# Mamba-2 scan and mixture of experts on one core: GpSimd waits for VectorE's turn on the shared port, first loads reordered and held back, sums of logarithms made in the opening

## The chip, the cores and the metric

The kernel runs on one core of a Trainium2 chip. The core has five engines with instruction queues of their own: TensorE (PE, matrix products from SBUF into PSUM; its weight loads are shown as PEld), VectorE (DVE), ScalarE (ACT), GpSimd (POOL) and SyncE (SP, which here issues nearly all DMAs). Engines wait for each other by semaphores; each works through its queue in order, so that one waiting instruction holds everything behind it. The metric is the device time of one execution in microseconds. Three executions of the kernel before gave 621.44, 622.16 and 623.01 us; the median is 622.16.

## The reference

Two blocks follow each other. The first is a state-space scan over 4 sequences and 8 heads, 768 positions each, head dimension 32, state dimension 16, in chunks (the kernel uses chunks of 128 positions, the result is the same):

```python
log_a = np.log(np.clip(a, 1e-06, 1.0))
cum = np.cumsum(la, axis=-1)                       # within a chunk
L = np.exp(cum[:, :, :, None] - cum[:, :, None, :]) * causal
M = np.einsum('bhin,bhjn->bhij', Cc, Bc) * L
y_intra = np.einsum('bhij,bhjd->bhid', M, xc)
y_inter = np.einsum('bhin,bhnd->bhid', Cc, state) * np.exp(cum)[:, :, :, None]
y[:, :, sl] = y_intra + y_inter
Bx = np.einsum('bhjn,bhjd->bhjnd', Bc, xc) * np.exp(cum[:, :, -1:] - cum)[:, :, :, None, None]
state = decay_full[:, :, None, None] * state + np.sum(Bx, axis=2)
```

The second is a mixture of four experts over the 3072 tokens of 256 values that the first makes, with hidden size 1024 and probabilities `p` normalised over the experts:

```python
for e in range(E):
    h = np.maximum(x @ w1[e], 0.0)
    out += p[:, e:e + 1] * (h @ w2[e])
```

All is float32.

## The kernel before

**Tiles.** The 24 chunks of 128 tokens are numbered so that four neighbours belong to the four sequences. A chunk's data come in `xb` (x, B and the transposes of B and C). The decay matrix of a chunk is made in one of two ways. For chunks 0 to 5 (`SCANNED`) DVE makes it by a running product of the decays (`scan`, L513 and L515), for chunks 0 to 2 from decays that PE has spread over the partitions, for 3 to 5 from a tile `ab` that a DMA spreads from the DRAM copy `acut_d` of the clipped decays (L457 to L460). For chunks 6 to 23 ACT makes it as an exponential (L522) of `ab`, spread from `cum_d`, the DRAM copy of the running sums of logarithms, minus the transposed sums `neg`; GpSimd then sets the upper triangle to zero (`causal`, L527). From chunk 4 on the state carried in is scaled by `dec` (L829: the exponential of `ah`, loaded from `cum_d` at L465) into `cts` (GpSimd, L831). PE multiplies C by B (`score`, L498), DVE multiplies the result by the decay matrix (L847), PE makes the outputs (L542 and, for the carried state, L870), ACT copies them out (L885 and L552), DVE transposes and carries the state (L901 and L903). `fade` (L536, GpSimd) scales B.

**The experts** are worked through in products of 128x256 blocks by a scheme with fewer products than the plain one. It needs sums of weight blocks (`w`, L1015, by GpSimd or DVE), sums of token blocks (`Y`, L1034, DVE), and sums of products (DVE: L951, L1062, L1251 and L1424). The first four chunk pairs' worth of work is done with smaller schemes: four plain products (`plain_first`), whose outputs go to the `own_` house, then two pairs of feature blocks (`twos`), then units of four feature blocks (`fours`) over blocks of six chunks. All products are issued at L924, each as a pair of matrix multiplications. ACT copies intermediate results out of PSUM (L933, L1204 and L1208) and back into it (L938); DVE applies the rectifier and the gate (L959). Sums of weights that later blocks need again are stored (`w_d`, L1020) and loaded again (L1004).

**What sets the order.** Up to L727 the order is the program's own: the opening. It loads the first tiles, clips the decays, makes chunks 0 and 1 and the gates; ACT copies the transposed gates at L643, and at L671 the scores that GpSimd multiplies; DVE multiplies the other scores at L677. From there on every piece of work is an entry (`Work`) with the engines that may do it, a duration in the planner's own cost table, and what it reads and writes. PE's entries stand in an order written out by hand (`line`). `Plan.run` then goes through time, and gives each free engine the ready entry with the earliest due time (`latest`), counted back from PE's order; it also chooses the tile. It knows DVE's and GpSimd's shared port: entries of DVE with `two` (both inputs in SBUF) and of GpSimd with `port` do not overlap in the plan (`self.port`). The instructions are issued in the order of planned starts (L1506 to L1509). On the chip only true dependencies make an engine wait, so that the plan's times do not hold anything back there.

**SP's queue.** SP issues the loads and stores in the planned order. Eight semaphores serve them in turn, so a DMA is not issued before the one eight places earlier has landed. The first part is the program's own: `xb` of chunks 0 and 1, two tiles of `w1` (L473), `xb` of chunk 2, the store of `acut_d` (L626), `xb` of chunk 3, `ab` of chunk 3, two more tiles of `w1`, four of `w2` (L479). From `p_d` (L727), the DRAM copy of the gates, on it is the plan's order.

**The sums of logarithms.** After the sixth entry of `line` (`MARK`) ACT takes the logarithm of the decays in place (L1378), DVE makes the running sums in two scans (L1380), SP stores them to `cum_d`. `bias()` transposes them by PE into `neg`; it stands after the fifth of the `twos` products (L1413 to L1415).

Of the kernel before, what the change touches and what calls it, by code (L numbers as in the profile page):

```python
# [36 lines left out]
SCORED, OWN, LEAD, LEFT, MARK = 5, 3, 5, 3, 5  # L37
FILLED = 3
ORDERS = (0, 1, 2, 3), (3, 1, 2, 0), (0, 1, 2, 3), (3, 1, 2, 0)
# [29 lines left out]
class Plan:  # L69
# [109 lines left out]
    def run(self, line, at, begin):  # L179
# [19 lines left out]
        while todo:  # L199
# [4 lines left out]
            for w in waiting[e]:  # L204
                if w.start is not None or e == "PE" and w.place != head:
                    continue
# [149 lines left out]
def kernel(  # L356
# [100 lines left out]
    def load_decays(c, ab):  # L457
        src = acut_d if c < SCANNED else cum_d
        nc.sync.dma_start(
            out=ab, in_=src[real(c)].rearrange("h s -> (h s)").partition_broadcast(P))  # L460
# [16 lines left out]
    def load_w2(fb, w):  # L477
        e, f = divmod(fb, EPB)
        nc.sync.dma_start(  # L479
            out=w.rearrange("p (j m) -> p j m", j=JJ),  # L480
            in_=w2[e, f * FB:f * FB + FB].rearrange("(j p) m -> p j m", p=P))
# [149 lines left out]
    load_decays(3, homes["ab"][0])  # L631
    for fb in range(2, 4):
        load_w1(fb, homes["W"][fb])
    for fb in range(4):
        load_w2(fb, homes["W"][4 + fb])

# [66 lines left out]
    turn_gates(BANK[7])  # L703
    next_ = [BANK[4], BANK[0], BANK[1], BANK[6]]
# [11 lines left out]
    for r in (3, 1, 2):  # L716
        masked(1, r, MT[1], LT[1], next_[r], 0)
    ys = []
# [52 lines left out]
    la = plan.taken("cum", 0, now)  # L771
    cum, neg, cd = value("cum"), value("neg"), value("dram")
    cd.dram = True
# [598 lines left out]
    for seq, _ in plain[:2]:  # L1372
        line.extend(seq)
    scores([2, 3])
    for seq, _ in plain[2:]:
        line.extend(seq)
    mark = line[MARK]
    act(.42, lambda e: nc.scalar.activation(out=la.t, in_=la.t, func=AF.Ln), part=[la], after=mark)  # L1378
    for r in range(2):
        dve(.6, lambda e, r=r: nc.vector.tensor_tensor_scan(  # L1380
            out=cum.t[:, r], data0=la.t[:, r], data1=zeros[:NCH * NH // 2], initial=0.0,
            op0=ALU.add, op1=ALU.add), two=True, reads=[la], part=[cum], after=mark)
    dma(lambda e: store_decays(nc.sync, cum_d, cum.t), kb=96, reads=[cum], part=[cd])
# [29 lines left out]
    line.extend(rest[:5])  # L1413
    bias()
    line.extend(rest[5:])  # L1415
# [86 lines left out]
    for i, w in enumerate(leave_last(len(blocks) - 1, O, LAST)):  # L1502
# [3 lines left out]
    done = plan.run(line, now, {"PE": now, "DVE": now - .6, "ACT": now + 1.0, "POOL": now - 2.0,  # L1506
                                "SP": now + 1.0})
    for w in done:
        w.fn(w.by)  # L1509

# [44 lines left out]
```

## Time and profile before

| | us |
|---|---|
| median of three executions (621.44 to 623.01) | 622.16 |
| the profiled execution's own time | 624.35 |
| its span, first to last instruction | 622.6 |
| PE busy in the span | 606.6 |
| DVE busy | 498.7 |
| ACT busy | 291.7 |
| GpSimd busy | 180.9 |
| DVE busy in the window 13 to 150 (137 us) | 121.3 |
| GpSimd busy in the window 13 to 150 | 91.3 |

In the lines of the profile, `L924 PE MATMUL bank<-v,w ... x8` is an operation of PE that was written in line 924, reads tiles `v` and `w` and writes `bank`, eight times. In a timeline the first number is the start, the second the length of the group; in brackets stands how long the engine was idle before it and what ended that. A list of waits gives the time in total, the number of times and the longest. PE's matrix multiplications are pipelined: one of 128x256 in float32 lasts 381 ns, and the next starts 216 ns after it; each product at L924 makes four. PEclk is the granted clock of PE in tenths, in 40 slices of the span of 15.6 us each.

### The profile page before, as it was taken

What the parts mean: (1) busy time and instruction counts of PE and PEld (TensorE: products, weight loads), DVE (VectorE), ACT (ScalarE), POOL (GpSimd) and SP (SyncE); (2) the same over time, 40 slices, a digit from 0 to 9 for tenths busy, and PEclk for the clock granted to TensorE, in tenths of its full rate; (3) what the DMA queues carried; (4) which work ended last, traced back from release to release, by engine and by line L of the source; (5) the groups of instructions that cost most, each with busy time, mean ns of one, the idle gap of its engine ahead of it and who ended that gap; (6) DMA issues with size and microseconds to landing.
All of it is one profiled execution on the core that took longest, in us unless ns stands there. A gap on an engine that the chain in (4) does not pass through costs nothing.

```text
span 622.6 us, 10073 instructions
## 1 busy us (share of the span) xinstructions
PE 606.6 (97%) x3365; PEld 515.1 (83%) x3365; DVE 498.7 (80%) x852; ACT 291.7 (47%) x681; POOL 180.9 (29%) x240
## 2 busy tenths in 40 slices
PE   9979989989999999999999999999999999999997
PEld 5757868868888888888888888888888888888885
DVE  6879897998879987497877989487695988576675
ACT  4247627357662325867534332855435142444441
POOL 6586962973262110696700110110000000000000
PEclk9999989999999999999999999999999999999999
DMA  6968538636772526976352332974233232974001
GB/s 185 322 211 269 176 110 274 218 125 220 271 249 68 163 35 183 326 263 239 102 159 78 106 103 50 298 247 141 82 93 94 83 103 34 307 232 130 1 0 52
DMA packets 89060, 99.65 MB, mean 160 GB/s; under 512 B 27428, under 2 KB 58928, under 8 KB 89008
## 3 DMA queue, kind: packets, MB, share of 16 engines
q1 hardware_dynamic: 88852, 98.95, 50.7%
q8 instruction: 27, 0.44, 0.3%
q14 instruction: 25, 0.20, 0.1%
q10 hardware_dynamic: 156, 0.06, 0.0%
HBM read 78.80 MB, written 20.17 MB: 159 GB/s over the span
## 4 chain that ended last, share of the span: by engine, by line
PE 82%; DVE 8%; DMA 5%; issue 2%; POOL 1%; ACT 1%; SPq 0%; DVEq 0%; POOLq 0%; ACTq 0%
PE bank L924 79%; DVE v L951 2%; DVE v L959 1%; DMA ah<-cum_d 1%; DMA ab<-acut_d 1%; POOL w L1015 1%; DMA w<-in_w_dram 1%; PE bank L498 1%; PE bank L542 1%; DVE Y L1034 1%; DMA acut_d<-v 1%; DVE w L1015 1%; DVE MT L847 1%; DMA ab<-cum_d 1%; PE bank L870 0%
## 5 line engine op out<-in xcount | busy, mean ns | idle before, releaser
L924 PE MATMUL bank<-v,w 128*128 128x256 f32 x1672 | 394.7, 381 | 5.2 <-DVE v L959 2.5
L924 PEld LDWEIGHTS bank<-v,w 128*128 128x128 f32 x1672 | 317.3, 191 | 53.0 <-issue 4.8
L924 PE MATMUL bank<-Y,w 128*128 128x256 f32 x692 | 177.7, 381 | 4.2 <-DVE bank L1062 1.8
L924 PEld LDWEIGHTS bank<-Y,w 128*128 128x128 f32 x692 | 130.0, 190 | 26.1 <-DVE bank L1062 2.4
L1204 ACT COPY v<-bank 128x512 f32<-128x512 f32 x107 | 62.6, 585 | 180.6 <-PE bank L924 168.5
L959 DVE SCALAR_TENSOR_TENSOR v<-bank,gate 128x512 f32<-128x512 f32 x144 | 98.5, 686 | 43.3 <-PE bank L924 41.1
L951 DVE TENSOR_TENSOR v<-v,v 128x512 f32<-128x512 f32 x175 | 128.6, 753 | 1.2
L1015 POOL TENSOR_TENSOR w<-w,w 128x256 f32<-128x256 f32 x95 | 81.8, 882 | 34.4 <-PE bank L924 21.7
L1062 DVE TENSOR_TENSOR bank<-bank,v 128x512 f32<-128x512 f32 x86 | 58.6, 695 | 34.1 <-PE bank L924 23.2
L933 ACT COPY v<-bank 128x512 f32<-128x512 f32 x102 | 59.6, 586 | 55.2 <-PE bank L924 44.5
L938 ACT COPY bank<-v 128x512 f32<-128x512 f32 x129 | 74.5, 591 | 12.3 <-DVE v L959 8.7
L924 PE MATMUL bank<-LT,w 128*128 128x256 f32 x212 | 54.0, 380 | 0.0
L527 POOL TENSOR_SCALAR_AFFINE_SELECT MT<-MT 128x512 f32<-128x512 f32 x36 | 25.6, 724 | 80.0 <-ACT MT L522 75.2
L522 ACT ACTIVATE MT<-ab,neg 128x128 f32<-128x128 f32 x144 | 46.4, 392 | 0.0
L924 PEld LDWEIGHTS bank<-LT,w 128*128 128x128 f32 x212 | 40.1, 190 | 6.0 <-DVE v L959 0.3
L1015 POOL TENSOR_TENSOR w<-w 128x256 f32<-128x256 f32 x32 | 27.0, 853 | 18.0 <-PE bank L924 12.3
L951 DVE TENSOR_TENSOR v<-bank,v 128x512 f32<-128x512 f32 x26 | 17.9, 690 | 10.6 <-PE bank L924 8.1
L951 POOL TENSOR_TENSOR v<-v,v 128x512 f32<-128x512 f32 x4 | 8.1, 2031 | 51.2 <-DVE v L959 51.1
L847 DVE TENSOR_TENSOR MT<-bank,MT 128x512 f32<-128x512 f32 x36 | 22.8, 679 | 0.0
L491 ACT ACTIVATE ctm<-xb,tmask 128x128 f32<-128x128 f32 x48 | 15.8, 391 | 10.3 <-DMA xb<-in_xbc_dram 10.0
L1251 DVE TENSOR_TENSOR v<-v,v 128x256 f32<-128x256 f32 x51 | 19.9, 425 | 0.8 <-ACT v L1204 0.5
L959 DVE SCALAR_TENSOR_TENSOR v<-v,gate 128x512 f32<-128x512 f32 x26 | 18.8, 724 | 0.4
(119 smaller groups left out, 335.6 us busy)
## 6 DMA issues: line engine op xcount, KB each, us to landing
w<-w_d SPq DMA_DIRECT2D x128, 256.0 KB
w_d<-w SPq DMA_DIRECT2D x64, 256.0 KB
w<-in_w_dram SPq DMA_DIRECT2D x40, 256.0 KB
ab<-cum_d SPq DMA_DIRECT2D x18, 512.0 KB
w<-in_w_dram SPq DMA_DIRECT2D x64, 128.0 KB
gate<-p_d SPq DMA_DIRECT2D x15, 384.0 KB
xb<-in_xbc_dram SPq DMA_DIRECT2D x17, 192.0 KB
xb<-in_xbc_dram SPq DMA_DIRECT2D x7, 320.0 KB
```

Of the source, the lines that this page charges most:

```text
L522: nc.scalar.activation(out=MT[:, place(c, h), 0:P], in_=ab[:, h * P:h * P + P], func=AF.Exp, bias=neg[:, h % NT, NQ * real(c) + h // NT:NQ ...
L527: nc.gpsimd.affine_select(out=MT[:, h:h + n, 0:P], in_=MT[:, h:h + n, 0:P], compare_op=ALU.is_ge, fill=0.0, base=0, pattern=[[0, n], [1, P ...
L847: nc.vector.tensor_mul(to, g, LT0[:, js, h] if cs[0] < SCANNED else to)
L924: nc.tensor.matmul(out=o, lhsT=w[:, j], rhs=x if half is None else x[:, j], start=(start and j == 0), stop=(j == 1), skip_group_check=True)
L933: act(.5, lambda e: nc.scalar.copy(out=flat(v), in_=bank.t), reads=[bank], writes=[v])
L938: act(.54 if to - lo > FB else .32, lambda e: nc.scalar.copy(out=bank.t[:, lo:to], in_=flat(v)[:, lo:to]), reads=[v], writes=[bank])
L951: plan.add(engines, lambda e: (on(e).tensor_add if sign > 0 else on(e).tensor_sub)(flat(v), whole(x), whole(y)), reads=[x, y], writes=[v], ...
L959: dve(D512, lambda e: nc.vector.scalar_tensor_tensor(out=h.t, in0=whole(x).rearrange("p (j m) -> p j m", j=JJ), scalar=0.0, in1=g.t[:, 2 * ...
L1015: plan.add(B256, lambda e, r=r, x=x, y=y, sign=sign: (on(e).tensor_add if sign > 0 else on(e).tensor_sub)(view(r), view(x), view(y)), two= ...
L1062: dve(D512, lambda e: (nc.vector.tensor_add if sign > 0 else nc.vector.tensor_sub)(to.t, bank.t, whole(x)), reads=[x, bank], writes=[to])
L1204: act(.5, lambda e: nc.scalar.copy(out=flat(v), in_=bank.t), reads=[bank], writes=[v], hold=HOLD)
L1251: plan.add(engines, lambda e: (on(e).tensor_add if sign > 0 else on(e).tensor_sub)(o[1](), x[1](), y[1]()), reads=[v for v in vs if v is n ...
```

## The change

There are three parts. First, the instructions are issued as before, but a GpSimd operation that uses the port, if it is the first since the last such DVE operation in the issue order, now waits for that DVE operation to end; DVE does not wait in turn. Second, the load of `ab` for chunk 3 moves behind the six weight loads, and the planner leaves a load alone, in its first 80 us (`OPENING`), as long as its due time is more than 26 us away (`HORIZON`). The start times that the planner assumes for DVE and SP move a little (`now - .2` and `LOADED`). Third, logarithm, running sums and the store of `cum_d` move into the opening, after `turn_gates` and after the masking of chunk 1; `bias()` moves ahead of the scores of chunks 2 and 3. `OWN` goes from 3 to 2: one product fewer of the first house stands ahead of the outputs of chunks 2 and 3. The planner runs again with all this, so that the order on DVE, ACT, GpSimd and SP, the tiles that are used and the engine of a few sums differ throughout.

```diff
--- before.py
+++ after.py
@@ -34,8 +34,9 @@
 LEAN = 4.0
 EASY = 40.0
 SCANNED = 6
-SCORED, OWN, LEAD, LEFT, MARK = 5, 3, 5, 3, 5
+SCORED, OWN, LEAD, LEFT = 5, 2, 5, 3
 FILLED = 3
+HORIZON, OPENING, LOADED = 26.0, 80.0, 1.0
 ORDERS = (0, 1, 2, 3), (3, 1, 2, 0), (0, 1, 2, 3), (3, 1, 2, 0)
 PAIRS_AT = ((1, 24, "s0"), (2, 1, "o0"), (2, 1, "s1"), (2, 24, "s2"), (3, 1, "o12")), (
     (1, 1, "s0"), (1, 24, "s1"), (2, 1, "o01"), (2, 24, "s2"), (3, 1, "o2"))
@@ -203,6 +204,9 @@
             late = self.late = max(0.0, t["PE"] - line[head].nominal) if head < len(line) else 0.0
             for w in waiting[e]:
                 if w.start is not None or e == "PE" and w.place != head:
+                    continue
+                if w.kb and now < OPENING and w.latest + late > now + HORIZON:
+                    soon = w.latest + late - HORIZON if soon is None else min(soon, w.latest + late - HORIZON)
                     continue
                 ready = max([w.ready, w.after.nominal + late if w.after else 0.0] + [
                     n.end + ((MARGIN if now < SURE or w.latest + late < now + 8 else LEEWAY) if n.kb and e != "SP" else -n.lag if n.by == e == "PE" else HOP)
@@ -628,11 +632,11 @@
 
     store_decays(nc.sync, acut_d, a_cut)
     load_tokens(3, xb[3])
-    load_decays(3, homes["ab"][0])
     for fb in range(2, 4):
         load_w1(fb, homes["W"][fb])
     for fb in range(4):
         load_w2(fb, homes["W"][4 + fb])
+    load_decays(3, homes["ab"][0])
 
     BANK = homes["bank"]
     rows = NCH * E
@@ -701,6 +705,7 @@
     for r in (2, 3):
         masked(0, r, MT[0], LT[0], seven[r], 0)
     turn_gates(BANK[7])
+    nc.scalar.activation(out=a_sb, in_=a_sb, func=AF.Ln)
     next_ = [BANK[4], BANK[0], BANK[1], BANK[6]]
     scan_quarters(1, LT[1], four, 0)
     score([1], ctm[1:], xb[1:2], next_)
@@ -715,6 +720,12 @@
     spread_gate(BANK[5], homes["gate"][0])
     for r in (3, 1, 2):
         masked(1, r, MT[1], LT[1], next_[r], 0)
+    sums = homes["cum"][1]
+    for r in range(2):
+        nc.vector.tensor_tensor_scan(
+            out=sums[:, r], data0=a_sb[:, r], data1=zeros[:NCH * NH // 2], initial=0.0,
+            op0=ALU.add, op1=ALU.add)
+    store_decays(nc.sync, cum_d, sums)
     ys = []
     for t in range(NT):
         y = BANK[6 + t][:, :P + N]
@@ -768,9 +779,7 @@
         st[c]["A"] = plan.taken("A", c, now)
     g0 = gates[0, 0] = plan.taken("gate", 0, now)
     LTv = [plan.taken("V", i, now) for i in range(4)]
-    la = plan.taken("cum", 0, now)
-    cum, neg, cd = value("cum"), value("neg"), value("dram")
-    cd.dram = True
+    cum, cd, neg = plan.taken("cum", 1, now), plan.taken("dram", 0, now + 3.0), value("neg")
 
     def fetch(c):
         s = st[c]
@@ -1371,16 +1380,10 @@
     decays(3)
     for seq, _ in plain[:2]:
         line.extend(seq)
+    bias()
     scores([2, 3])
     for seq, _ in plain[2:]:
         line.extend(seq)
-    mark = line[MARK]
-    act(.42, lambda e: nc.scalar.activation(out=la.t, in_=la.t, func=AF.Ln), part=[la], after=mark)
-    for r in range(2):
-        dve(.6, lambda e, r=r: nc.vector.tensor_tensor_scan(
-            out=cum.t[:, r], data0=la.t[:, r], data1=zeros[:NCH * NH // 2], initial=0.0,
-            op0=ALU.add, op1=ALU.add), two=True, reads=[la], part=[cum], after=mark)
-    dma(lambda e: store_decays(nc.sync, cum_d, cum.t), kb=96, reads=[cum], part=[cd])
     dma(lambda _: nc.sync.dma_start(
         out=g0.t[:, 4:6], in_=p_d[0, 4:6].rearrange("c s -> (c s)").partition_broadcast(P).rearrange(
             "p (c s) -> p c s", s=P)), kb=128, part=[g0])
@@ -1410,9 +1413,7 @@
     back = {acc: (r,) for r, acc in PUT.items()}
     groups = [(two, {r: t for r, t in twos_right(h).items() if r != 1}) for two, (_, h) in zip(twos, made)]
     behind = second(0, "S", groups, FIRST_HOUSES, put=back)
-    line.extend(rest[:5])
-    bias()
-    line.extend(rest[5:])
+    line.extend(rest)
 
     def fold():
 
@@ -1503,10 +1504,18 @@
         behind.insert(len(behind) - TAILS[i], w)
     line.extend(behind)
 
-    done = plan.run(line, now, {"PE": now, "DVE": now - .6, "ACT": now + 1.0, "POOL": now - 2.0,
-                                "SP": now + 1.0})
+    done = plan.run(line, now, {"PE": now, "DVE": now - .2, "ACT": now + 1.0, "POOL": now - 2.0,
+                                "SP": now + LOADED})
+    traced, turn = nc.cur_bb.bb.instructions, None
     for w in done:
+        n = len(traced)
         w.fn(w.by)
+        if w.by == "DVE" and w.two:
+            turn = traced[-1]
+        elif w.by == "POOL" and w.port and turn is not None:
+            tc.add_manual_dep(traced[n], turn.name, mybir.DependencyInfo(
+                mybir.DependencyClass.Sync, mybir.DependencyReason.DATA), reason="shared port")
+            turn = None
 
 
 # ---- launch: one core; numpy lays the inputs out, and nothing else ----
```

## The prediction

> **What bounds the kernel now.** I read the page's busy shares and slices first, then the waits of TensorE (PE), the chain that ended last, and timelines and windows of the stretches in which PE stops. The page, and then PE's waits by what ended them:
>
> ```profile
> span 622.6 us, 10073 instructions
> ...
> PE 606.6 (97%) x3365; PEld 515.1 (83%) x3365; DVE 498.7 (80%) x852; ACT 291.7 (47%) x681; POOL 180.9 (29%) x240
> ...
> PEclk9999989999999999999999999999999999999999
> ```
>
> ```profile
> engine line waited for: us in total, times, longest us
> PE bank L924 <- DVE v L959: 2.5, 3, 1.8
> PE bank L924 <- POOL w L1015: 2.0, 1, 2.0
> ```
>
> PE is the bound: from 140 us to 612 us its matmuls start 216 ns apart with one stop of 0.14 us. So nothing that the change does after 140 us can win; what can be won is the stops between 13 and 140 us, 10.0 us of idle PE, plus about 0.16 us of pipeline restart at each of eleven, plus what the clock does after the longest. Where they lie, from the timeline of PE:
>
> ```profile
> 18.58 6.28 PE L924 MATMUL bank<-v,w 128*128 128x256 f32 x28 [0.62 <-DMA w<-in_w_dram]
> ...
> 34.66 1.99 PE L924 MATMUL bank<-v,w 128*128 128x256 f32 x8 [1.79 <-DVE v L959]
> 37.56 0.67 PE L870 MATMUL bank<-cts,S 32*32 32x256 f32 x16 [0.90 <-ACT v L1208]
> ...
> 43.51 4.80 PE L924 MATMUL bank<-Y,w 128*128 128x256 f32 x20 [1.38 <-DVE Y L1034]
> ...
> 79.98 4.51 PE L924 MATMUL bank<-v,w 128*128 128x256 f32 x12 [2.05 <-POOL w L1015]
> ...
> 140.05 1.13 PE L924 MATMUL bank<-Y,w 128*128 128x256 f32 x4 [1.77 <-DVE bank L1062]
> ```
>
> The 12 matmuls at 79.98 take 4.51 us where 12 x 0.216 + 0.16 = 2.75 are due: 1.76 us lost to the clock (the sixth PEclk slice is the only one under 9; the window 80 to 83.5 shows 0.51). What stands behind the first four stops is told by the chain:
>
> ```profile
> 6.49 4.89 DMA acut_d<-v
> 11.77 6.68 DMA w<-in_w_dram
> ...
> 24.18 7.41 DMA ab<-acut_d
> ...
> 35.96 4.17 DMA ah<-cum_d
> ```
>
> They are loads issued late: SP stood until 11.40 at the load of `ab` for chunk 3, which waits for the store of `acut_d`, with six weight loads behind it, and everything later in the queue is late by that. Meanwhile the DMA engines were 0.36, 0.06 and 0.53 busy in the three microseconds from 10.
>
> **The change, part by part.** PE's own order is the same but for the two transposes of `bias` (0.33 us, moved from 48 to after the second plain unit) and one product of the first output house (moved past two chunks' outputs), so PE has the same work and only its stops can differ.
>
> *First loads.* The six weight loads now stand ahead of the `ab` load. SP is free at 7.3 (6.87 + 0.43), each issue takes 0.47, so they go out from 7.3 to about 10.5 and use the idle engines; the stop of 0.62 goes. The `ab` load is issued at 11.40 as before, since `acut_d` lands then, but now behind 1.57 MB. At 312 to 379 GB/s (windows 17 to 19) these and its own 0.52 MB take 5.5 to 6.7 us from 10.4: 15.9 to 17.1. DVE scans it at 17.02. From the far side, the loaded load of 7.41 us would land it at 18.8, 1.8 late, of which DVE's idle 0.64 before 20.59 takes a part. I take 0.2 us lost, ends 0 and 1.2.
>
> *Sums of logarithms.* The logarithm (0.40, L1378) goes into ACT's idle 0.81 before 9.77. The two scans (1.54, L1380) follow the masking that ends at 11.85 on DVE and end at 13.4; behind them stand the transposes of the carried state, of which the second starts at 13.66 anyway, after 1.69 idle. Cost 0; if GpSimd's sums of 11.53 to 13.6 hold the scans up, at most 0.4. In exchange the store of `cum_d` leaves SP at some 13.7 instead of 25.75, and the `ah` loads (32.29 to 34.14) go out ten microseconds earlier; their 4.17 us then end near 25, before ACT needs them.
>
> *The three stops that follow.* With SP some 4 us ahead, the third `ab` load (24.18) goes out at 20 to 22 (not before the scan of chunk 3 frees its tile at 19.95). With the same 7.41 it lands at 27.4 to 29.4 instead of 31.6. Its scans (2.26), a Y sum (0.34) and two of the score products (L847, 0.60 each), which now stand ahead of the gates, end at 31.2 to 33.2, and the gate that PE waits for (0.67) at 31.9 to 33.9; it began at 33.94 before. PE would want it at 32.6, so the 1.79 becomes 0 to 1.3; I count 1.4 won. The 0.90 goes, since the outputs of chunks 4 and 5 now use banks other than the one that L1208 empties. The 1.38 came from ACT: a `dec` that waited for `ah` until 40.13 stood ahead of the copies at 40.43 that feed the Y sums. In the new order these copies come first; the three Y sums still meet GpSimd, so I count 1.1 of 1.38. Together 0.62 + 1.4 + 0.9 + 1.1 + three restarts 0.5 - 0.2 = 4.3 us.
>
> *The stop at 77.9.* It waits for a GpSimd sum of weights that ended at 79.97. Before it, GpSimd stood idle for ACT 4.51 us at the causal masks (L527), and the masks of four chunks stood ahead of the last eight sums:
>
> ```profile
> 60.09 0.74 POOL L527 TENSOR_SCALAR_AFFINE_SELECT MT<-MT 128x512 f32<-128x512 f32 x1 [4.51 <-ACT MT L522]
> ...
> 72.17 4.44 POOL L1015 TENSOR_TENSOR w<-w,w 128x256 f32<-128x256 f32 x4
> ```
>
> In the new order all 19 sums from the first stored one to the one that PE waits for stand ahead of the first L527. They can begin when the last early fade is done, near 30 (32.98 before); 19 x 0.90 (the mean in 13 to 150) ends at 47, and PE comes near 73. That cover of 26 us holds with every added wait. Won: 2.05 + 0.16 + 1.76 = 4.0 us.
>
> *GpSimd's waits for the port.* In the built order 118 of GpSimd's rows wait for DVE, 27 before: 91 waits. What they can win is DVE's time in contention, here for the Y sums (DVE's timeline, then GpSimd's):
>
> ```profile
> 42.52 2.67 DVE L1034 TENSOR_TENSOR Y<-v,Y 128x256 f32<-128x256 f32 x3
> 45.11 0.41 DVE L1034 TENSOR_TENSOR Y<-Y,Y 128x256 f32<-128x256 f32 x1
> ```
>
> ```profile
> 41.41 2.63 POOL L1015 TENSOR_TENSOR w<-w 128x256 f32<-128x256 f32 x3
> ```
>
> A pair of them takes 0.87 (start to start 41.65, 42.52); alone DVE steps 0.34 and GpSimd 0.69, 1.03 in all. So they overlap by 0.16, and whoever comes first, the other waits. A GpSimd operation that waits for one DVE operation meets the next, which does not wait for it, so in a dense run both still alternate; only the places that GpSimd took ahead of its turn come back. Stops that are DVE's or ACT's in all: 0.72 at 51 to 53, 0.94 in three, 1.77 at 138. Ends: nothing, and 3.4 won. I take 0.5, near the lower end, as the row shows alternation. Queued behind a waiting GpSimd operation are all its later sums, masks and `cts`, and behind these SP's stores of sums; PE waits for them. A wait costs between 0 and 0.53 (0.94 - 0.41); I take 0.5 us in all, as GpSimd was idle a third of 13 to 150 (91 of 137 busy).
>
> [...]
>
> *What comes late next.* PE is then some 8 us early at 84, and DVE has no idle time from 83.67 to 100.1. The 4.0 won at 78 meet 1.36 of DVE idle in 80 to 85 and 1.6 of contention (three operations longer by 0.53); the rest, 1.0, I give back, ends 0 and 2.6. `HORIZON` holds loads back to 26 us before their due time; the longest load here took 7.41, so it costs nothing.
>
> Sum: 4.3 + 4.0 + 0.5 - 0.5 - 1.0 = 7.3 us. The profiled execution took 624.35 (span 622.6), 2.2 above the median 622.16; it should come to 617.0 and the median to 614.9.
>
> **Rivals.**
> - *DVE takes it back.* DVE is 121.3 of 137 busy in 13 to 150. If it stays continuous behind the earlier PE, the stop at 78 is replaced by DVE's: only the opening's part survives, 4.3 less the 0.5: 618.4. For: no DVE idle from 41 to 64 and 84 to 100. Against: 4.6 us idle from 100 to 112, on PE.
> - *The opening wins little.* `ab` of chunk 3 lands 1.2 late and the third stays on the path: 4.3 falls to 1.0 and the rest to 3.0, 618.2.
> - *The waits do nothing to DVE.* Then 0.5 is missing: 615.4, not told apart.
> - *Slower: GpSimd late.* Between 72.17 and 89.03 it made 18 sums with 1.3 us idle. If each first waits out a DVE operation of 0.68, the next unit's sums are 12.2 us late and the clock halves once more (1.76): 614.9 + 14.0 = 628.9. It decides from a lateness of about 7 us. Against: PE did not stop for GpSimd there, and the sums now begin earlier.
>
> [...]
>
> **How the numbers follow.** Main case 0.50, 610.5 to 617.5 (from the ends above: 2.9 + 1.0 + 0.5 more won, or 1.0 + 1.6 less); DVE 0.18; opening 0.15; both together, about no change, 0.06; GpSimd late 0.11. The range 610.5 to 621.8 leaves out the last and little else. A measurement of this kernel tells 0.3% (1.9 us) from no change. Faster 0.83, same 0.06, slower 0.11.
>
> **What the next profile would show.** Right: no stop of PE at `w` loads, at L870 or for GpSimd in 70 to 80, PEclk 9 throughout, `cum_d` issued before 15 us, 140.05's matmul near 132. Wrong: a wait of PE for L1015's sums of over 2 us, POOL's idle time released by DVE, DVE waiting at 17 us for `ab` for over 1 us, or new DVE stops in 84 to 110.

## The result, and the profile after

The changed kernel took 614.74 us (median of 4 executions, 614.24 to 617.03), the kernel before 622.59 us beside it (621.44 to 623.97): a ratio of 0.988, 95% interval 0.9848 to 0.9913. The forecast was 614.9, so the number came out. The reasons did not; most of what follows is about that.

The page of the changed kernel (its profiled execution took 617.03 us; it holds a stretch at half clock, from 27.39 to 30.80 us (granted clock 0.50), which lowers its mean granted clock to 0.997; the other three stand at 0.999 and lie within 0.6 us of each other):

```profile
span 615.3 us, 10136 instructions
...
PE 605.7 (98%) x3365; PEld 514.8 (84%) x3365; DVE 489.5 (80%) x854; ACT 292.5 (48%) x681; POOL 157.6 (26%) x238
...
PEclk9899999999999999999999999999999999999999
```

PE has the same 3365 matmuls. Both engines that the planner has on the shared port are busy for less: DVE 489.5 in place of 498.7 us, POOL 157.6 in place of 180.9, with nearly the same work. What PE waited for (engine and line, what released it, us in total, times, longest):

```profile
engine line waited for: us in total, times, longest us
PE bank L546 <- POOL w L1024: 1.4, 1, 1.4
...
PE bank L933 <- DVE bank L1071: 0.8, 1, 0.8
...
PE bank L546 <- DVE MT L856: 0.7, 1, 0.7
PE bank L933 <- ACT LT L894: 0.4, 1, 0.4
```

The timeline of PE shows where these lie (start, busy time, what, and in brackets the idle time ahead of it):

```profile
24.98 0.41 PE L546 MATMUL bank<-MT,xb 128*32 128x144 f32 x2 [1.36 <-POOL w L1024]
26.08 1.18 PE L546 MATMUL bank<-MT,xb 128*32 128x144 f32 x30 [0.70 <-DVE MT L856]
...
77.31 2.83 PE L933 MATMUL bank<-v,w 128*128 128x256 f32 x12 [0.80 <-DVE bank L1071]
```

Every stop that the forecast showed is gone or small (79.98 with its 2.05 for GpSimd is now 77.31 with 0.80 for VectorE; those of 0.62, 1.79, 0.90, 1.38 and 1.77 are gone), and there is a new pair at 25. Stops of over 0.3 us between 13 and 150 us fell from 9.85 to 3.62 us in all. The same matmuls of PE in the two timelines show in which stretch the time was won:

| matmul that began, before | after | earlier by | won in the stretch before it |
|---|---|---|---|
| 43.51 | 42.86 | 0.65 | 0.65 (forecast: 4.3) |
| 84.33 | 79.97 | 4.36 | 3.7 (forecast: 4.0) |
| 111.21 | 106.86 | 4.35 | 0.0 (forecast: 1.0 given back) |
| 140.05 | 132.97 | 7.08 | 2.7 (forecast: nothing by itself) |

The 0.65 is what is left after the half clock at 27.39, which cost about 1.76 (an estimate from the 12 matmuls at 79.98 in the kernel before, 4.51 us for 2.75); the 3.7 contains the 1.76 of the half clock at 79.98 in the kernel before. After that both run nearly alike: the matmul behind PE's last stop begins 7.30 us earlier (606.61 for 613.91). So the sum agrees with the forecast, and three of its four stretches don't.

### The profile page after: what moved, and what is told of

It is laid out like the page before. It is cut to its first block, busy times and chain, and to the rows that moved or that the text cites. A ratio compares the mean times of both kernels' runs of the same rounds, so it can differ in the third digit from the quotient of the medians.

```text
span 615.3 us, 10136 instructions
## 1 busy us (share of the span) xinstructions
PE 605.7 (98%) x3365; PEld 514.8 (84%) x3365; DVE 489.5 (80%) x854; ACT 292.5 (48%) x681; POOL 157.6 (26%) x238
## 4 chain that ended last, share of the span: by engine, by line
PE 92%; DVE 2%; ACT 1%; issue 0%; DVEq 0%
PE bank L933 88%; PE bank L546 2%; PE bank L502 1%; PE bank L879 1%; DVE v L960 1%; DVE v L968 1%; ACT A L556 1%; DVE MT L856 0%; ACT v L894 0%; DVE bank L1071 0%; DVE v L1260 0%; PE bank L1325 0%; DVE v L1425 0%; ACT LT L894 0%; ACT v L1330 0%
## 5 line engine op out<-in xcount | busy, mean ns | idle before, releaser
L933 PE MATMUL bank<-v,w 128*128 128x256 f32 x1716 | 402.0, 381 | 1.1 <-DVE bank L1071 0.8
L933 PEld LDWEIGHTS bank<-v,w 128*128 128x128 f32 x1716 | 325.7, 191 | 50.0 <-issue 2.9
L1024 POOL TENSOR_TENSOR w<-w,w 128x256 f32<-128x256 f32 x94 | 72.1, 784 | 46.0 <-DVE v L960 13.8
L1071 DVE TENSOR_TENSOR bank<-bank,v 128x512 f32<-128x512 f32 x81 | 55.5, 696 | 35.2 <-PE bank L933 23.6
L947 ACT COPY bank<-v 128x512 f32<-128x512 f32 x126 | 73.2, 594 | 10.8 <-DVE v L968 8.7
L933 PE MATMUL bank<-LT,w 128*128 128x256 f32 x168 | 42.6, 380 | 0.0
L933 PEld LDWEIGHTS bank<-LT,w 128*128 128x128 f32 x168 | 31.8, 190 | 4.6 <-DVE v L968 0.3
L1024 POOL TENSOR_TENSOR w<-w 128x256 f32<-128x256 f32 x32 | 24.2, 762 | 23.2 <-DVE Y L1043 9.0
L1260 DVE TENSOR_TENSOR v<-v,v 128x256 f32<-128x256 f32 x58 | 22.9, 431 | 1.1 <-ACT v L1213 0.7
L856 DVE TENSOR_TENSOR MT<-bank,MT 128x512 f32<-128x512 f32 x36 | 22.7, 681 | 0.1
L1213 ACT COPY LT<-bank 128x512 f32<-128x512 f32 x12 | 7.0, 586 | 23.5 <-PE bank L933 23.5
L840 POOL TENSOR_TENSOR cts<-ctm,dec 128x256 f32<-128x256 f32 x20 | 14.5, 734 | 11.6 <-DVE v L960 5.1
```

The lines of the kernel that those rows point to most:

```text
L856: nc.vector.tensor_mul(to, g, LT0[:, js, h] if cs[0] < SCANNED else to)
L933: nc.tensor.matmul(out=o, lhsT=w[:, j], rhs=x if half is None else x[:, j], start=(start and j == 0), stop=(j == 1), skip_group_check=True)
L947: act(.54 if to - lo > FB else .32, lambda e: nc.scalar.copy(out=bank.t[:, lo:to], in_=flat(v)[:, lo:to]), reads=[v], writes=[bank])
L1024: plan.add(B256, lambda e, r=r, x=x, y=y, sign=sign: (on(e).tensor_add if sign > 0 else on(e).tensor_sub)(view(r), view(x), view(y)), two= ...
L1071: dve(D512, lambda e: (nc.vector.tensor_add if sign > 0 else nc.vector.tensor_sub)(to.t, bank.t, whole(x)), reads=[x, bank], writes=[to])
L1213: act(.5, lambda e: nc.scalar.copy(out=flat(v), in_=bank.t), reads=[bank], writes=[v], hold=HOLD)
```

## Experiments

Each run has the kernel before beside it on the same chip. Chips differ a little (before took 622.47 to 623.27 us on three of them), so the ratio to the kernel before is the number to compare; it goes by means, so it differs a little from the quotient of the medians.

| run | edit | us, median | ratio to before, 95% interval |
|---|---|---|---|
| (the change) | | 614.74 | 0.988 (0.9848 to 0.9913) |
| no_waits | change without GpSimd's waits | 628.35 | 1.0093 (1.0076 to 1.0109) |
| only_waits | before with GpSimd's waits | 616.26 | 0.9908 (0.9893 to 0.9923) |
| ab_first | change, order of first loads undone | 617.51 | 0.9912 (0.9894 to 0.993) |
| ab_mid | change, `ab` behind two weight loads, not six | 614.34 | 0.9871 (0.9858 to 0.9885) |
| logs_back | change, sums of logarithms back in the plan | 618.35 | 0.991 (0.9892 to 0.9928) |
| no_horizon | change without the holding back of loads | 615.07 | 0.9863 (0.9844 to 0.9881) |
| only_order | before with the order of first loads | 625.24 | 1.0027 (1.0009 to 1.0045) |
| waits_early | change, waits planned before 60 us only | 622.22 | 0.9981 (0.9968 to 0.9994) |
| waits_late | change, waits planned from 60 us only | 618.39 | 0.9934 (0.9919 to 0.995) |
| waits_from28 | change, waits planned from 28 us only | 614.61 | 0.9876 (0.9859 to 0.9893) |
| older_turn | change, wait for the turn before the last | 614.94 | 0.9858 (0.984 to 0.9876) |
| far_turn | change, wait for the fifth last turn | 616.29 | 0.9911 (0.989 to 0.9932) |

Two small parts of the change were not run by themselves: `OWN` and the planned start of VectorE. `LOADED` is 1.0, the value that SP's start had before, so it moves nothing.

### Which part carries the gain: no_waits and only_waits

The first leaves out of the changed kernel the lines that add the waits, and the second adds those lines alone to the kernel before:

```diff
-        if w.by == "DVE" and w.two:
-            turn = traced[-1]
-        elif w.by == "POOL" and w.port and turn is not None:
-            tc.add_manual_dep(traced[n], turn.name, mybir.DependencyInfo(
...
-            turn = None
```

> The changed kernel with its planned order, loads and sums, but GpSimd does not wait for VectorE. Theory (the loads and the planned order carry most of the 7.8 us, the waits about as much as the stops that went at 118 and 138, some 2.5): 616.5 to 618, VectorE's sums of 128x512 back from a mean of 720 ns to about 750, and PE stops again for VectorE near 132. Rival 1 (the waits carry it all): 621 or more. Rival 2 (as the prediction had it, in a dense run both alternate anyway and the waits do nothing): 614.2 to 615.3.

> The kernel before with its own order and loads, and only the waits of GpSimd added. Theory: the stop at 138 and part of the smaller ones go, the stops up to 44 us stay, the one at 78 stays (GpSimd's sums stand behind its masks): 619 to 621. Rival 1 (the waits carry it all): 615 to 617. Rival 2 (they do nothing): 622 to 623. Rival 3 (GpSimd gets late, the stop at 78 grows past 2 us): over 623.

In both the value is that of Rival 1. Without the waits the rest of the change makes the kernel 0.9% slower than before; the waits alone bring 0.9% of the change's 1.2%. Within the new order the waits are worth 13.6 us (628.35 less 614.74; 13.3 by the ratios), in the old one 6.2 (5.7 by the ratios). The forecast had 0.5 for them, less 0.5 of cost.

The page of only_waits, with the stop that is left near 75 us, and then the page of no_waits and its waits of PE:

```profile
PE 604.1 (98%) x3365; PEld 514.0 (84%) x3365; DVE 485.3 (79%) x852; ACT 291.8 (48%) x681; POOL 160.1 (26%) x240
...
75.73 2.83 PE L924 MATMUL bank<-v,w 128*128 128x256 f32 x12 [0.69 <-POOL MT L527]
```

```profile
PE 609.6 (97%) x3365; PEld 517.0 (83%) x3365; DVE 507.9 (81%) x854; ACT 292.0 (47%) x681; POOL 181.9 (29%) x238
```

```profile
PE bank L933 <- DVE v L968: 3.0, 1, 3.0
PE bank L933 <- DVE MT L856: 2.4, 1, 2.4
PE bank L933 <- DVE bank L1071: 2.0, 1, 2.0
PE bank L933 <- POOL w L1024: 1.8, 1, 1.8
```

Stops between 13 and 150 us come to 10.89 us against 3.62, and there are three stretches at half clock (granted clock 0.50) in place of one. Each cost about 1.76 us (from the 12 matmuls at 79.98 before): 7.27 + 2 x 1.76 = 10.8, where the two profiled executions differ by 11.3. Three of the four large stops are VectorE's, and it was busy 18.4 us longer than with the waits, with the same work.

### What the waits do: the same work with and without them

The clearest view is one in which only the waits differ. In waits_early the operations that the plan starts from 60 us on have none. The timelines of DVE and of GpSimd there:

```profile
84.09 1.22 DVE L960 TENSOR_TENSOR v<-v,v 128x512 f32<-128x512 f32 x1
85.23 0.94 DVE L1425 TENSOR_TENSOR v<-v,v 128x256 f32<-128x256 f32 x1
86.10 2.34 DVE L960 TENSOR_TENSOR v<-v,v 128x512 f32<-128x512 f32 x2
88.36 1.21 DVE L960 TENSOR_TENSOR LT<-v,LT 128x512 f32<-128x512 f32 x1
89.50 0.94 DVE L1024 TENSOR_TENSOR w<-w,w 128x256 f32<-128x256 f32 x1
90.36 2.47 DVE L856 TENSOR_TENSOR MT<-bank,MT 128x512 f32<-128x512 f32 x4
```

```profile
84.72 6.99 POOL L1024 TENSOR_TENSOR w<-w,w 128x256 f32<-128x256 f32 x7
```

And the same operations in the changed kernel, DVE and then GpSimd:

```profile
83.95 0.68 DVE L960 TENSOR_TENSOR v<-v,v 128x512 f32<-128x512 f32 x1
84.55 0.41 DVE L1425 TENSOR_TENSOR v<-v,v 128x256 f32<-128x256 f32 x1
84.89 1.28 DVE L960 TENSOR_TENSOR v<-v,v 128x512 f32<-128x512 f32 x2
86.09 0.68 DVE L960 TENSOR_TENSOR LT<-v,LT 128x512 f32<-128x512 f32 x1
86.69 0.41 DVE L1024 TENSOR_TENSOR w<-w,w 128x256 f32<-128x256 f32 x1
87.03 2.47 DVE L856 TENSOR_TENSOR MT<-bank,MT 128x512 f32<-128x512 f32 x4
```

```profile
87.25 1.41 POOL L1024 TENSOR_TENSOR w<-w,w 128x256 f32<-128x256 f32 x2 [3.50 <-DVE w L1024]
88.62 0.74 POOL L1024 TENSOR_TENSOR w<-w 128x256 f32<-128x256 f32 x1
```

Without waits GpSimd makes seven sums in a row, and VectorE's run of six operations alternates with them: 0.94 for 0.41, 1.21 for 0.68, some 0.53 each, and the four products of L856 begin 6.27 us after the run's start. With the wait GpSimd stands still for 3.50 us, until the run's last operation, and the products begin 3.08 us after the start. Three of the sums that GpSimd then makes lie beside the four products, which read one operand from a bank of PSUM, and cost VectorE nothing: the products take 2.47 us in both, with GpSimd's sums beside all four of them or, in waits_early, beside the first two (its seventh sum ends at 91.71). (The fourth, at 89.30, meets the next `v<-v,v` at 89.42, which takes 1.17.) Over the whole of 13 to 150 us a `MT<-bank,MT` takes 675 ns without the waits (no_waits) and 679 with them, a `v<-bank,gate` 682 and 686, but a `v<-v,v` of 128x512 takes 879 and 733.

So the wait doesn't exchange one loss for another. The plan had put GpSimd's operation behind the run, the chip ran it beside the run (84.72 to 91.71 in waits_early), and the wait brings the chip back to the plan (87.25 in the change). Port is the planner's name; the runs show which operations take longer beside each other, and not why.

### Where they win: waits_early and waits_late

```diff
-        elif w.by == "POOL" and w.port and turn is not None:
+        elif w.by == "POOL" and w.port and turn is not None and w.start < 60.0:
```

(and `w.start >= 60.0` in waits_late)

> Edit: after, with waits only for GpSimd operations that the plan starts before 60 us. Without any waits the stops of TensorE of 1.8, 2.4 and 2.0 us lay behind 60 us, with one half clock of about 1.7 us for each, and one stop of 3.0 us with its half clock before. Theory (the waits are worth something wherever GpSimd's sums meet a dense run of VectorE; the late ones carry some two thirds): 620 to 625, with stops of TensorE for VectorE or GpSimd between 75 and 145 us. Rival (the waits of the opening decide: once TensorE, VectorE and GpSimd are in step at 60 us the rest has enough slack): 614 to 616.5.

> Edit: after, with waits only for GpSimd operations that the plan starts at 60 us or later (the complement of the run with waits only before 60 us, which gave back 7.5 us). Without any wait the stops before 60 us were one of 3.0 us for VectorE with a half clock of about 1.7 behind it. Theory (the two halves add up: 13.6 between all and none, 7.5 for the late ones, so about 6 for the early ones): 618.5 to 622, with a stop of TensorE for VectorE near 48 us. Rival (the early ones do little by themselves, as the later stretch takes up a late start): 614.3 to 616.5.

waits_early: 622.22, as the theory had it, with the three stops that it names, from the timeline of its PE:

```profile
76.87 2.83 PE L933 MATMUL bank<-v,w 128*128 128x256 f32 x12 [1.75 <-DVE bank L1071]
...
91.09 1.13 PE L933 MATMUL bank<-v,w 128*128 128x256 f32 x4 [1.87 <-DVE MT L856]
...
136.78 1.21 PE L933 MATMUL bank<-Y,w 128*128 128x256 f32 x4 [1.96 <-DVE bank L1071]
```

The second is that of the run shown above. waits_late: 618.39, 0.1 us under the theory's range, with the stop that it names near 48 us:

```profile
50.69 3.58 PE L933 MATMUL bank<-v,w 128*128 128x256 f32 x8 [2.41 <-DVE v L968]
```

Missing late waits cost 7.5 us (6.3 by the ratios) and missing early ones 3.7 (3.4); all of them 13.6 (13.3). So the waits pay in both halves. The two add up to some 11 of 13.6 (9.7 of 13.3 by the ratios); where the rest comes from was not tested.

### How exact the wait must be: older_turn and far_turn

```diff
         if w.by == "DVE" and w.two:
-            turn = traced[-1]
-        elif w.by == "POOL" and w.port and turn is not None:
+            older, turn = turn, traced[-1]
+        elif w.by == "POOL" and w.port and older is not None:
...
-            turn = None
+            older = None
```

(in far_turn the operation named is the fifth last)

> Edit: after, but each GpSimd operation waits for the VectorE operation on the port before the last one that stands ahead of it, so about as many waits, each satisfied one VectorE operation earlier. Without the waits the two engines meet, and a VectorE sum of 128x256 takes 0.94 us in place of 0.41, one of 128x512 1.21 in place of 0.68: 0.53 for each meeting. Theory (the wait wins because GpSimd begins only when the very operation ahead of it is done, so that it falls into VectorE's idle time or behind its dense run): each waiting operation now meets one VectorE operation more, VectorE's busy time rises from 489 us by 10 or more, and a part of the 13.6 us between with and without waits is lost: 618 to 624. Rival (it is enough to keep GpSimd from running ahead by several operations; one more or less does nothing): 614 to 616.5.

> Edit: after, but each GpSimd operation waits only for the fifth last VectorE operation on the port ahead of it, so it may begin up to four of them before its turn. With the wait one VectorE operation earlier the time was the same as after. Theory (what the wait prevents is that GpSimd runs its sums beside a dense run of some six to eight VectorE sums, 0.53 us each; four ahead lets half of them meet again): 617 to 623, VectorE's busy time 494 to 502 us. Rival (any hold is enough): 614.3 to 616, VectorE's busy time under 492.

older_turn is as fast as the change; the theory that it must be the very last operation fell. Its page:

```profile
PE 603.9 (98%) x3365; PEld 513.9 (84%) x3365; DVE 488.9 (80%) x854; ACT 292.2 (48%) x681; POOL 172.0 (28%) x238
```

VectorE is busy no longer than with the exact wait (488.9 and 489.5), but GpSimd is, by 14.4 us. It is now released when the last operation of the run begins, comes second, and is the one that takes longer: two of its sums that begin at 90.31, just behind a `v<-v,v` of 90.28, take 1.92 us (two take 1.41 at 87.25 in the change), and the `v<-v,v` 0.67, no longer than in the change's run (0.68). GpSimd's mean sum `w<-w,w` grew from 784 to 867 ns, and GpSimd, busy 28% of the span, has time to spare.

far_turn lets GpSimd in four turns early. VectorE was busy 498.3 us, as the theory expected (494 to 502), but the time came to 616.29, under its 617 to 623 and just over the rival's 616, and at 0.9911 it is some 2 us slower than waits_from28 of the same chip (0.9876), whose late waits are exact; the two intervals just overlap. So VectorE's first 9 us of contention cost some 2 us and its next 10, in no_waits, 12. That fits a lateness that is hidden as long as PE has work ahead of it, but this was not tested.

### The opening: only_order, ab_first, ab_mid, logs_back, no_horizon

Order of loads alone, in the kernel before; ab_first undoes the same two lines in the change:

```diff
     load_tokens(3, xb[3])
-    load_decays(3, homes["ab"][0])
     for fb in range(2, 4):
         load_w1(fb, homes["W"][fb])
     for fb in range(4):
         load_w2(fb, homes["W"][4 + fb])
+    load_decays(3, homes["ab"][0])
```

> Edit: before, with the load of ab for chunk 3 behind the six weight loads and nothing else; no waits, no horizon, sums of logarithms in the plan. Theory (the first loads by themselves win next to nothing, since loads that come earlier only start GpSimd's sums earlier, beside VectorE's; with the sums of logarithms added to them and no waits the kernel came to 628): 621 to 625. Rival (the forecast's: the stop of 0.62 at 18 us and a good part of the three stops behind it go): 618.5 to 620.5.

> The changed kernel with the load of ab for chunk 3 back ahead of the six weight loads. Theory: VectorE's wait of 1.90 us for ab at 17.2 goes, and with it PE's stops of 2.06 us before the outputs of chunks 2 and 3 at 25 to 26; in exchange the weights go out from 11.2 again and PE stops some 0.6 for the third of them near 18: 612.8 to 613.8, and no half clock near 27. Rival (that stop is GpSimd's own lateness from its waits, ab has nothing to do with it): 615 to 616, since only the 0.6 is added.

only_order: 625.24, just over the theory's range and slower than before by 0.27%, where the forecast's account needed 618.5 to 620.5. The stops of 0.62, 1.79 and 1.38 did go (the stops before 45 us fall from 4.69 to 1.62), and the gain went into the next one. Its timelines of PE, of DVE and of GpSimd:

```profile
51.91 0.80 PE L924 MATMUL bank<-v,w 128*128 128x256 f32 x1 [3.71 <-DVE v L959]
```

```profile
43.87 1.81 DVE L1034 TENSOR_TENSOR Y<-Y,v 128x256 f32<-128x256 f32 x2
45.61 0.94 DVE L1424 TENSOR_TENSOR v<-v 128x256 f32<-128x256 f32 x1
...
47.93 1.26 DVE L951 TENSOR_TENSOR v<-v,v 128x512 f32<-128x512 f32 x1
49.12 0.94 DVE L1034 TENSOR_TENSOR Y<-Y,v 128x256 f32<-128x256 f32 x1
```

```profile
46.55 2.10 POOL L1015 TENSOR_TENSOR w<-w,w 128x256 f32<-128x256 f32 x3 [0.28 <-PE bank L924]
48.60 2.04 POOL L1015 TENSOR_TENSOR w<-w 128x256 f32<-128x256 f32 x2
```

There the Y sums take 0.94 in place of 0.41, beside GpSimd's sums. The 3.71 at 48 replaces 0.53 in the kernel before. The sums of logarithms don't mend that: no_waits, which has them too, stops there for 3.0. The 0.27% goes with half clocks: the executions of only_order with a granted clock of 1.0 took 621.3 to 622.3 us, those of the kernel before beside them 621.1 to 623.1.

ab_first: 617.51, no better than the waits alone, and 3.7 us over its expectation. Its profile is of the slowest of six executions (620.03 us). SP stands at the load of `ab` again, the six weight loads go out after it, and so the whole queue is late: the `ab` load of chunk 5 goes out at 25.85 (22.75 in the change), VectorE waits 2.57 us for it before its scan of 32.11, and PE stops for 2.81 at 33.8, with half clock behind it: the eight matmuls at 36.62 take 3.78 us (eight take 1.99 in ab_mid), and the mean granted clock is 0.994, the change's 0.997. My expectation looked only at the first of the loads.

> The changed kernel with the load of ab for chunk 3 behind two of the six weight loads, ahead of the other four. Theory: ab has 0.5 MB instead of 1.6 MB ahead of it and lands some 3 us earlier, near 16, before VectorE asks at 17.2; the two weights that PE needs at 18 still go out at 7.2: no stop at 18 and none at 25 to 26: 612.2 to 613.2. Rival (the stop at 25 is GpSimd's own): 614.5 to 615.2, no change.

ab_mid: 614.34, just under the rival's range; against the change's 614.74 no difference can be told. What it does is visible: VectorE no longer waits for that `ab`, and of the stops of 1.36 and 0.70 at 25 us 0.37 is left. But VectorE then waits 1.03 us for a later `ab`, at 28 us, and PE stops for 0.81 at 32.8, where the change has no stop. In the kernels with `ab` behind six weight loads the wait for the first was 1.0 (waits_late) to 2.7 us (older_turn), from one execution to another. The wait of VectorE in the change:

```profile
DVE LT L519 <- DMA ab<-acut_d: 1.9, 1, 1.9
```

PE's stop at 25 us goes with it: 0.4 to 0.7 us where the wait was 1.0 to 1.2, 1.36 at 1.9, 1.8 to 2.5 at 2.5, 2.23 at 2.7.

> Edit: after, with waits only for GpSimd operations that the plan starts at 28 us or later. In the profile of after GpSimd's sum of 20.43 us waits for VectorE's scan, which waits 1.9 us for the load of ab; TensorE then stops for GpSimd 1.4 us at 25, and a half clock of 3.4 us follows. Theory (there the wait passes a late load on to GpSimd and so to TensorE, and costs more than it wins): this stop goes, 612.8 to 614.3. Rival (without the early waits GpSimd holds VectorE up before 28 us and the stop comes back as one for VectorE, or the load is what TensorE waits for anyway): 614.4 to 616.5.

waits_from28 was to show that this stop is passed on by a wait. It isn't: without the waits before 28 us it stands at 1.80, with `ab` 2.5 us late. The load itself is the cause, by way of VectorE's scans and the masked products behind them; the profile names GpSimd, but in the change GpSimd's product for these outputs (L540) had ended at 23.49, and VectorE's masked products (L856) at 24.83, just before PE began at 24.98.

The sums of logarithms back in the plan, and the holding back of loads switched off:

```diff
-    nc.scalar.activation(out=a_sb, in_=a_sb, func=AF.Ln)
...
-    store_decays(nc.sync, cum_d, sums)
...
+    act(.42, lambda e: nc.scalar.activation(out=la.t, in_=la.t, func=AF.Ln), part=[la], after=mark)
...
+    dma(lambda e: store_decays(nc.sync, cum_d, cum.t), kb=96, reads=[cum], part=[cd])
```

```diff
-HORIZON, OPENING, LOADED = 26.0, 80.0, 1.0
+HORIZON, OPENING, LOADED = 26.0, 0.0, 1.0
```

> Edit: after with the sums of logarithms back in the plan (logarithm, two scans, store of cum_d and place of the bias as before); waits, order of loads and horizon stay. Theory (with the waits there, the other parts are worth about 1.5 us together, 616.3 with the waits alone against 614.7, and the loads a half of it): 614.8 to 616.5. Rival (the forecast's: the early store of cum_d and the early loads behind it carry 1 to 2 us of stops between 33 and 44 us): 616.7 to 618.5, with stops of TensorE in 33 to 44 us of 1 us or more.

> Edit: after with the rule that keeps a load back to 26 us before its due time switched off. Theory (the longest load took 7.4 us, so holding back costs and wins nothing): 614.2 to 615.4. Rival (without it loads go out early and stand ahead of those that the opening needs, in SP's queue or on the DMA engines; or the plan that results is another): 616 or more, with VectorE or TensorE waiting for a load between 17 and 45 us longer than the 1.9 us for ab at 17.

logs_back: 618.35, the rival's value, and of its two stops one lies where the rival put it. From its waits of PE and from SP's timeline:

```profile
PE bank L546 <- DVE MT L851: 2.5, 1, 2.5
PE bank L874 <- POOL cts L835: 1.6, 1, 1.6
```

```profile
26.71 0.32 SPq L630 DMA_DIRECT2D cum_d<-cum  x1
28.63 1.85 SPq L469 DMA_DIRECT2D ah<-cum_d  x3
```

`cum_d` goes out at 26.71 and not at 12.63, the `ah` loads follow it (19.29 in the change), ScalarE makes its `dec` of them at 35.06 (22.27 in the change) and GpSimd the `cts` at 37.37, for which PE stops at 36.5. Whether `dec` came late by the loads or by the new plan's order the trace does not tell. The last 0.55 us ahead of that `cts` is, by the code, an added wait, for a transpose of VectorE (L905) that the `cts` does not read: here a wait cost PE time. The other stop, at 22.7, is that of the late `ab` (2.5 us). no_horizon: 615.07, as the theory had it: holding loads back does nothing that can be measured here.

So with the waits in place the order of the loads without the sums of logarithms (logs_back, 0.991) and the sums without the order (ab_first, 0.9912) each win nothing over the waits alone (0.9908). Together they do: 0.9863 in no_horizon beside logs_back, 0.9871 in ab_mid beside ab_first, with intervals that don't touch, some 2 to 3 us. (no_horizon stands there for the change, whose own interval is wider and overlaps with all of these.) logs_back and no_horizon are planned anew, so that more than the named part differs in them; what of the 2 to 3 us is the sums' own, and what the order's that the planner then found, is not separated.

## Why the prediction was right, and where it was wrong

The number (614.9 for 614.74) and the matmul "near 132" (132.97) were right, but by a sum in which two terms failed in opposite directions: the opening won 3.7 us less than forecast, and the waits, priced at nothing net, won what was missing. That the sum came out is luck.

- *First loads, sums, the three stops that follow: 4.3 forecast, 0.65 in the profile.* The stops named did go, as did the wait at L870, and `cum_d` left SP at 12.63 (before 15, as forecast); the two scans cost nothing, as VectorE waited for `ab` behind them. What failed is the step "I take 0.2 us lost, ends 0 and 1.2" for `ab`: it was issued at 11.23 and scanned at 19.13, VectorE waited 1.9 us, and PE stopped 1.36 and 0.70 at 25, with half a clock behind it in this one execution. Without that half clock (1.76) the opening wins 2.4. The second failure is larger: these terms were taken as won for good. only_order shows that, without the waits, they are lost again by 52 us.
- *The stop at 77.9: 4.0 forecast, 3.7 in its stretch.* The size was right and the reason wrong. It said that with 19 sums ahead of the first mask a cover of 26 us holds. The order alone doesn't do it: no_waits has the same order and stops 1.83 us for a GpSimd sum at 78.6. The waits do it: only_waits has the old order of the masks and stops 0.69 there. The term also took a half clock of 1.76 off the median: of the 45 executions of the kernel before that stand beside the experiments, 25 have a granted clock of 1.0 and so had no such stretch. For these the term was 2.2.
- *GpSimd's waits: 0.5 won, 0.5 cost, in the forecast.* This is the step that failed: "A GpSimd operation that waits for one DVE operation meets the next, which does not wait for it, so in a dense run both still alternate". It took a row of alternation (0.87 for a pair) as what would remain. But the wait names the last operation of a run, as the plan has it, so the whole run is clean (0.41 and 0.68 us in the change from 83.95 on), and the next VectorE operations often read a bank of PSUM and take no longer beside GpSimd's sums (679 ns with the waits, 675 without, for a `MT<-bank,MT`). The far end that I gave, 3.4, was also too small: it counted the stops named after VectorE and ScalarE alone, while the waits also shorten GpSimd's stop at 78 (0.69 in only_waits) and spare the half clocks behind such stops. Measured: 6.2 alone, 13.6 in the new order. Nor did I count what it is worth to move a loss to GpSimd. In older_turn GpSimd is busy 14.4 us longer than in the change, at the same time (614.94 and 614.74, 628.35 without waits): a loss moved to an engine that is busy a quarter of the time (28% of the span there) is a gain.
- *Given back: 1.0 forecast, nothing measured* (4.36 before the stretch, 4.35 behind it). Then 2.7 more were won at the stops of 0.38 at 117 and 1.77 at 138, which the forecast counted only in the waits' far end of 3.4. Both are gone in the change. The second is contention on VectorE: without the waits it is back with 1.97 (no_waits). The first is gone with the waits alone and without them alike (only_waits, no_waits), so what it came from stays open.
- *The signs.* Right: no stop at `w` loads, at L870, for GpSimd in 70 to 80. Signs of failure that came though the number stood: VectorE's wait for `ab` was over 1 us, and PEclk has an 8. "POOL's idle time released by DVE", which I gave as a sign of failure, is the very thing that wins: groups of GpSimd's sums that wait 4 to 18 us in all for VectorE stand in the profile, and no stop of PE but that of 25 us, which is the load's, names GpSimd.
- *The rivals.* "DVE takes it back" did come without the waits (stops of 3.0, 2.4 and 2.0 for VectorE in no_waits); with them 0.80 at 77 is left of it. "The waits do nothing to DVE" is refuted by its 13.4 us less busy time with the waits alone. "The opening wins little" did happen, with `ab` even later than its 1.2, and the waits made up for it. "GpSimd late" didn't come: GpSimd had time, busy for 157.6 us in place of 180.9.

## What to carry to other kernels

When operations of two engines take longer beside each other and one of the engines has time to spare, a wait that puts the idle one behind the busy one's dense runs can be a gain, as here, even if it then stands still for long. Before pricing such contention, sort the busy engine's operations by whether the trace shows them longer beside the other's (here a `v<-v,v` of 128x512, 879 ns without the waits and 733 with them) or not (`MT<-bank,MT`, 675 and 679): the second kind is where the other engine's work can go. And don't sum up gains of an opening as won until the next dense stretch has been looked at: what comes earlier may only meet something sooner.

## What the runs showed of the hardware that I had not expected

**In these runs a half clock went with where a stop lay on a grid, not with its length alone.** The three slow stretches of no_waits begin at 51.00, 95.38 and 143.16 us. They are 44.38 and 47.78 us apart, 13.00 and 14.00 times 3.413 us (47.78 divided by 14), and each lasts one such step. Two in only_order, at 51.46 and 82.18, are 30.72 apart, 9.00 steps. Windows of that grid in no_waits: the one ahead of each slow stretch, the slow one, and one with a stop of 1.83 us that brought none (window, its length, busy time of PE, PEld, DVE, ACT and POOL, granted clock, DMA share, GB/s):

```profile
47.59:51.00 3.41, 0.89 (x5) 0.43 (x3) 3.38 (x7) 2.96 (x11) 3.21 (x4) 1.00 0.66 200
51.00:54.41 3.41, 2.92 (x7) 2.39 (x8) 2.14 (x5) 0.00 (x0) 0.33 (x1) 0.50 1.09 324
91.97:95.38 3.41, 1.05 (x5) 0.60 (x5) 3.41 (x5) 2.28 (x6) 3.05 (x4) 1.00 0.03 11
95.38:98.79 3.41, 3.41 (x9) 2.70 (x9) 3.34 (x6) 0.00 (x0) 0.00 (x0) 0.50 0.68 250
139.75:143.16 3.41, 1.44 (x7) 0.96 (x7) 3.41 (x5) 1.49 (x4) 3.41 (x4) 1.00 0.70 205
143.16:146.57 3.41, 3.41 (x10) 2.69 (x9) 3.36 (x9) 2.50 (x8) 1.36 (x2) 0.50 0.57 204
...
78.30:81.72 3.42, 1.59 (x8) 1.14 (x7) 3.42 (x7) 0.00 (x0) 3.42 (x6) 1.00 0.81 264
```

In the profiled executions in which the grid can be laid this way (no_waits, waits_early, only_order and the kernel before), the windows with a long stop and PE busy 0.14 to 1.45 us were followed by a half clock and those with 1.59 to 1.69 were not. In waits_early the stop of 2.00 us at 23.3 lies, by its grid, across a boundary at 25.02, 1.73 on one side, and brings none, while 1.96 at 134.8 lies in one window and brings one. One window doesn't fit: that of the changed kernel from 23.98 to 27.39, busy 1.72, was followed by one; most of what PE did there were narrow matmuls (32 of 33), and whether these count for less is open. The phase of the grid, counted from the span's start, was 3.2 us in no_waits, 1.6 in the kernel before and 0.1 in the change, so by my estimate the same stop of 2 us costs 2.0 or, with 1.76 for a half clock, 3.8. The spread of only_order goes with the clock: 621.3 to 622.3 us at a granted clock of 1.0, 623.9 to 625.3 at 0.997, 625.5 to 625.9 at 0.995. In ab_first the half clock lasted longer: behind the eight matmuls at 36.62 (3.78 us), without a stop of PE, the 16 at L879 take 1.10 us and the 32 at L546 1.83 (0.66 at 38.46 and 1.19 at 39.05 in the change); why stays open. The busiest of the windows up to 1.45 us, in waits_early, was idle for 57% of its 3.41; no run here shows what sets the clock.

**Which of the two engines takes longer could be chosen.** With the wait one operation early (older_turn) GpSimd was busy 14.4 us longer than in the change and VectorE 0.6 less, at the same time (614.94 and 614.74); without waits (no_waits) both were busy longer, by 24.3 and 18.4 us.
